# Attention scores in pieces of 32 keys on 64x32 tiles, and another order of row halves in the output products

## The chip, the cores and the metric

The kernel runs on one core of a Trainium2 chip. The metric is the device time of one execution in microseconds; the time before is the median of three runs.

## The reference

Two parts follow each other. A gated linear attention makes an output per token and head; a feed-forward block with an unusual activation takes these outputs as its input.

```python
# attention: 4 batches, 8 heads, 768 tokens, head size 48
state = zeros((B, H, D, D))
for t in range(S):
    state = alpha[:, :, t, :, None] * state + einsum('bhd,bhe->bhde', k[:, :, t], v[:, :, t])
    y[:, :, t] = einsum('bhd,bhde->bhe', q[:, :, t], state)
# feed-forward: 3072 tokens, 384 -> 2048 -> 384
x = y.transpose(0, 2, 1, 3).reshape(B * S, H * D)
h = x @ w_in
sp = maximum(h, 0) + log1p(exp(-abs(h)))
out = (h * erf(sp)) @ w_out
```

## The kernel before

**The attention** works on chunks of 64 tokens for two batches at once (NI = 2, i). There are 24 chunks; after every twelfth a new pair of batches begins. The eight heads stand as four pairs; the two heads of a pair (par) lie in the two halves of the 128 partitions, rows 0 to 47 and 64 to 111. (For the second batch the halves are swapped.) In a chunk the running product of alpha (A) goes into the queries (Q = q * A) and into the keys (K = k / A); then three groups of float32 products on TensorE do the work:

- scores, step a4, line 198: `pS = K^T Q`, 64 keys by 64 queries for each pair, batch and half: 16 products. VectorE multiplies the whole result with the causal mask (line 203) into sT.
- outputs, step a5, line 226: `py` sums, for both batches, the state's share (T with Q, 48 rows) and the chunk's own share (v with sT, 64 rows). Each product makes 32 columns of the output by 64 tokens, on a tile of 64 rows by 32 columns of TensorE's array that `tile_position=(r0, c0)` names. The row half r0 is where the operands lie; the column strip c0 is where the output lies. Heads of 48 columns are cut into pieces (PIECES) so that 32 columns fit a strip. A chunk has 64 such products, 32 where no state exists yet (the first chunk of a pair of batches).
- state updates, also in a5, line 237: `pu = k^T v`, 16 products on four 64x64 tiles, but for the last chunk of a pair of batches. Ahead of the scores, line 187 transposes K for them.

Then `put` (lines 274 and 275) turns py into the block's input x_hi and x_lo, and VectorE brings the state up to date (lines 250 to 255).

**The feed-forward** takes blocks of 256 tokens, two chunks of two batches each; there are twelve. H (line 310) makes h in float32r with three products for one (hi and lo parts), 128x128 weights by 256 tokens; U, L1, L2, G and Z are the activation, on ScalarE and VectorE; O (line 367) multiplies with w_out, 384 columns wide, into two accumulators.

**Order.** Each engine runs its instructions in program order. The order of the steps is written out by hand in three strings: START, then ORDER for each following block, then TAIL. In ORDER the attention of two coming chunks (`a1_0 ... a5_1`) is woven into the steps of this block, the block before (`@-1`) and the block after (`@1`). In steady state the scores of a chunk and its outputs are apart by half an H or more: `a4_0 H_0_0@1 ld_1 a5_0` and `a4_1 O_3_1@-1 H_2_0@1 L1_3 L2_2 H_2_1@1 a5_1`. In the scores the loop's innermost index is par, so the row half changes with each product; in the outputs it is i, with the row half `(par ^ i) * HD`, so that within four products the halves are 0, 64, 64, 0. The scores name no tile position: a product of up to 64 rows and 64 columns uses the 64x64 tile where its operands and its output lie.

Of the kernel before, what the change touches and what calls it, by code (L numbers as in the profile page):

```python
# [44 lines left out]
def gla_moe(ctx: ExitStack, tc: tile.TileContext, q, k, v, alpha, w_in, w_out, out):  # L45
    nc = tc.nc


    M, CPB, _, D, NP, NI, TC = q.shape
# [11 lines left out]
    HD = 64  # L61
# [25 lines left out]
    for i in range(NI):  # L87
        half = maskn[i * TC : (i + 1) * TC]
        nc.gpsimd.affine_select(
            out=half, in_=half, pattern=[[1, TC]], compare_op=ALU.is_ge, fill=0.0, base=0, channel_multiplier=-1  # L90
# [43 lines left out]
    class Chunk:  # L134
# [47 lines left out]
        def a4(self):  # L182
            K, Q = self.K, self.Q
            if not self.last:
                pn = ps_at.tile([P, 512], F32, name="pn", tag="at")
                for pair in range(NP):
                    nc.tensor.transpose(  # L187
                        pn[:, pair * P : (pair + 1) * P], K[:, pair].rearrange("p i t -> p (i t)"), ident
                    )
                self.kn = at.tile([P, NP, 2, HD], F32, name="kn", tag="kn", bufs=1)  # L190
                nc.scalar.activation(self.kn.rearrange("p a b d -> p (a b d)"), pn, AF.Copy)

            ps = ps_at.tile([P, NP * NI, TC], F32, name="pS", tag="at")
            for pair in range(NP):
                for i in range(NI):
                    for par in range(2):
                        rows = slice(par * HD, par * HD + D)
                        nc.tensor.matmul(  # L198
                            out=ps[par * HD : (par + 1) * HD, pair * NI + i, :],
                            lhsT=K[rows, pair, i, :], rhs=Q[rows, pair, i, :], start=True, stop=True,  # L200
                        )
            self.sT = at.tile([P, NP, NI, TC], F32, name="sT", tag="sT", bufs=1)
            nc.vector.tensor_tensor(
                out=self.sT.rearrange("p a i t -> p (a i) t"), in0=ps, in1=maskn.unsqueeze(1).broadcast_to([P, NP * NI, TC]), op=ALU.mult
            )

        def a5(self, moe):
            vx, vt = self.vv[:, : NI * NP * HD], self.vv[:, NI * NP * HD :]
            if self.n % 2 == 0:
                moe.alloc_x()  # L210

            py = [ps_at.tile([P, KT, TC], F32, name="py", tag="at") for _ in range(NI)]
            for kt in range(KT):
                sums = []
                for w, d0 in PIECES[kt]:
                    if not self.first:
                        sums.append((w, d0, T, D, self.Q))
                    sums.append((w, d0, vx, HD, self.sT))
                for n, (w, d0, left, rows, right) in enumerate(sums):
                    for part in range(2):  # L220
                        for par in range(2):
                            for i in range(NI):
                                r0, pair = (par ^ i) * HD, 2 * part + w
                                at0 = (i * NP + pair) * HD + d0
                                c0 = par * HD + part * 32
                                nc.tensor.matmul(  # L226
                                    out=py[i][c0 : c0 + 32, kt, :], lhsT=left[r0 : r0 + rows, at0 : at0 + 32],
                                    rhs=right[r0 : r0 + rows, pair, i, :], start=n == 0, stop=n == len(sums) - 1,
                                    tile_position=(r0, c0),
                                )  # L230
            if not self.last:
                pu = [ps_at.tile([P, 512], F32, name="pu", tag="at") for _ in range(NI)]
                for pair in range(NP):
                    for half in range(2):
                        for i in range(NI):
                            toks, h = slice(i * TC, (i + 1) * TC), 2 * pair + (half ^ i)
                            nc.tensor.matmul(  # L237
                                out=pu[i][half * HD : (half + 1) * HD, pair * D : (pair + 1) * D],
                                lhsT=self.kn[toks, pair, half, :], rhs=vt[toks, h * D : (h + 1) * D],
                                start=True, stop=True,  # L240
                            )
            moe.put(py, self.n % 2)
            if not self.last:
                ae = self.A[:, :, TC].rearrange("p (a i) -> p i a", a=NP)
                aeb = ae.unsqueeze(3).broadcast_to([P, NI, NP, D])
                for i in range(NI):
                    U = pu[i][:, : NP * D].rearrange("p (a d) -> p a d", a=NP)
                    if self.first:
                        nc.vector.scalar_tensor_tensor(
                            out=Tv[:, i], in0=U, scalar=-1.0, in1=aeb[:, i], op0=ALU.mult, op1=ALU.mult  # L250
                        )
                    else:
                        nc.vector.tensor_tensor(out=Tv[:, i], in0=Tv[:, i], in1=U, op=ALU.subtract)
                if not self.first:
                    nc.vector.tensor_tensor(out=Tv, in0=Tv, in1=aeb, op=ALU.mult)
# [272 lines left out]
    for i in range(1, NBLK):  # L528
# [6 lines left out]
        out=top[:, 0:2], in_=flags.rearrange("p n two -> p two n"), op=ALU.max, axis=mybir.AxisListType.X  # L535
# [67 lines left out]
```

## Time and profile before

| what | value |
|---|---|
| median of three runs | 584.02 us (581.95 to 585.95) |
| the profiled execution, its own time | 582.33 us |
| its span, from the first to the last instruction | 580.4 us |
| mean granted TensorE clock | 0.969 |
| busy: TensorE, its weight loads, VectorE, ScalarE | 90%, 85%, 83%, 81% |
| TensorE matmul records | 7386 |

The profile is of one execution. PE is TensorE's matmuls, PEld its weight loads, DVE VectorE, ACT ScalarE. A row of a group names the line, the engine, the operation, the tiles (output <- inputs), the number of records, the busy time and the mean of one. A float32 product of the code shows as two records, each a weight load and a matmul; a float32r product shows as one. The durations of records overlap, since the matmuls are pipelined: pace is read from the distance between starts. The view by stretches shows, for each stretch, its length, each engine's busy time and in parentheses the number of records that were under way in it, then the granted clock and the DMA share; where a line is named, it counts that line's records alone.

### The profile page before, as it was taken

To read this page: it belongs to the slowest core of one execution; us is meant where nothing else is said; L and a number is where in the kernel's file an instruction comes from. 1 tells how busy PE (TensorE), PEld (TensorE's weight loads), DVE (VectorE), ACT (ScalarE), POOL (GpSimd) and SP (SyncE) were. 2 spreads that over 40 slices of the span, in tenths; PEclk is the share of its full clock that TensorE was granted. 3 is DMA by queue.
4 is the path that set the end of the run, shared out by engine and by line. 5 is a ranking of instruction groups with operands and counts; after the bars stand their busy time and mean duration, and the time that the engine had idled before them with its cause. 6 is when DMAs were issued, how large, how long until landed. Compare 5 with 4: busy or idle time off the path is not lost.

```text
span 580.4 us, 16926 instructions
## 1 busy us (share of the span) xinstructions
PE 519.5 (90%) x7386; PEld 496.0 (85%) x7386; DVE 483.6 (83%) x688; ACT 468.6 (81%) x704; POOL 2.4 (0%) x16
## 2 busy tenths in 40 slices
PE   0588687499999999999999999999999999999584
PEld 0486686488989999999999999999999999999584
DVE  6779969999999979969789699699699698594970
ACT  4446799579999799699699798797896996989911
POOL 1000000000000000000000000000000000000000
PEclk9999799789999999999999999999999999999878
DMA  6575633522412222212202312221211100000000
GB/s 194 177 230 168 203 91 107 178 86 63 128 28 61 76 55 62 64 52 75 88 25 65 88 32 72 75 61 43 73 62 44 53 8 30 1 29 1 28 0 33
DMA packets 36370, 43.64 MB, mean 75 GB/s; under 512 B 21952, under 2 KB 25024, under 8 KB 36288
## 3 DMA queue, kind: packets, MB, share of 16 engines
q1 hardware_dynamic: 36288, 42.48, 24.3%
q8 instruction: 60, 0.98, 0.7%
q14 instruction: 22, 0.18, 0.1%
HBM read 37.75 MB, written 4.72 MB: 73 GB/s over the span
## 4 chain that ended last, share of the span: by engine, by line
PE 69%; DVE 15%; ACT 9%; issue 3%; DMA 2%; SPq 0%; ACTq 0%; DVEq 0%
PE acc L367 29%; PE ph L310 29%; PE py L226 4%; PE pS L198 3%; DVE wbuf L401 2%; DVE s L342 2%; ACT s L326 2%; PE pu L237 1%; PE pn L187 1%; DVE wbuf L404 1%; DVE A L156 1%; DVE t L334 1%; DVE w L335 1%; DVE hs L343 1%; ACT hs L315 1%
## 5 line engine op out<-in xcount | busy, mean ns | idle before, releaser
L310 PE MATMUL ph<-x_hi,wi_hi 128*128 128x256 f32 x576 | 166.9, 290 | 7.5 <-ACT wi_hi L379 4.8
L310 PE MATMUL ph<-x_lo,wi_hi 128*128 128x256 f32 x576 | 164.0, 285 | 0.0
L310 PE MATMUL ph<-x_hi,wi_lo 128*128 128x256 f32 x576 | 163.7, 285 | 0.3 <-DVE wi_lo L380 0.2
L367 PE MATMUL acc<-wo_hi,gh 128*128 128x384 f32 x384 | 133.2, 347 | 16.4 <-DVE gh L356 16.4
L367 PE MATMUL acc<-wo_hi,gl 128*128 128x384 f32 x384 | 131.4, 346 | 2.0 <-DVE gl L359 1.9
L367 PE MATMUL acc<-wo_lo,gh 128*128 128x384 f32 x384 | 131.0, 341 | 0.0
L310 PEld LDWEIGHTS ph<-x_hi,wi_hi 128*128 128x128 f32 x576 | 111.4, 194 | 10.1 <-ACT wi_hi L379 5.1
L359 DVE TENSOR_TENSOR gl<-hs,gh 128x512 fp32r<-128x512 f32 x96 | 64.9, 686 | 58.4 <-ACT gh L358 57.6
L310 PEld LDWEIGHTS ph<-x_hi,wi_lo 128*128 128x128 f32 x576 | 111.5, 194 | 1.0 <-DVE wi_lo L380 0.8
L310 PEld LDWEIGHTS ph<-x_lo,wi_hi 128*128 128x128 f32 x576 | 111.0, 193 | 0.5 <-DVE x_lo L275 0.3
L367 PEld LDWEIGHTS acc<-wo_hi,gh 128*128 128x128 f32 x384 | 73.8, 192 | 18.0 <-issue 8.7
L315 ACT ACTIVATE hs<-ph 128x512 f32<-128x512 f32 x96 | 56.3, 590 | 39.3 <-PE ph L310 38.1
L367 PEld LDWEIGHTS acc<-wo_hi,gl 128*128 128x128 f32 x384 | 72.7, 191 | 7.4 <-DVE gl L359 7.0
L367 PEld LDWEIGHTS acc<-wo_lo,gh 128*128 128x128 f32 x384 | 73.7, 192 | 0.0
L334 DVE TENSOR_TENSOR t<-s,w 128x1024 f32<-128x1024 f32 x48 | 58.5, 1218 | 1.9 <-ACT w L328 1.4
L335 DVE SCALAR_TENSOR_TENSOR w<-t,w 128x1024 f32<-128x1024 f32 x48 | 58.4, 1216 | 0.3
L358 ACT ACTIVATE gh<-hs 128x512 fp32r<-128x512 f32 x72 | 44.9, 625 | 16.3 <-PE acc L367 12.5
L343 DVE SCALAR_TENSOR_TENSOR hs<-s,hs 128x1024 f32<-128x1024 f32 x48 | 57.9, 1215 | 0.1
L342 DVE TENSOR_TENSOR s<-s,w 128x1024 f32<-128x1024 f32 x48 | 57.5, 1215 | 0.4 <-ACT s L338 0.4
L326 ACT ACTIVATE s<-s,fixed 128x1024 f32<-128x1024 f32 x48 | 54.6, 1141 | 0.0
L321 ACT ACTIVATE s<-hs 128x1024 f32<-128x1024 f32 x48 | 49.7, 1055 | 1.6 <-DVE wbuf L398 0.9
L328 ACT ACTIVATE w<-w 128x1024 f32<-128x1024 f32 x48 | 50.4, 1051 | 0.3
(62 smaller groups left out, 715.1 us busy)
## 6 DMA issues: line engine op xcount, KB each, us to landing
raw_v<-in_v_dram SPq DMA_DIRECT2D x24, 448.0 KB, 3.7
wst<-in_moe_w_in_dram SPq DMA_DIRECT2D x12, 512.0 KB, 5.7
wst<-in_moe_w_out_dram SPq DMA_DIRECT2D x16, 384.0 KB, 3.7
raw_a<-in_alpha_dram SPq DMA_DIRECT2D x48, 96.0 KB, 2.9
raw_k<-in_k_dram SPq DMA_DIRECT2D x48, 96.0 KB, 2.2
raw_q<-in_q_dram SPq DMA_DIRECT2D x48, 96.0 KB, 2.3
out_dram<-o SPq DMA_DIRECT2D x24, 192.0 KB, 1.9
```

Source lines behind the costliest of these rows:

```text
L310: nc.tensor.matmul(out=o, lhsT=wt[:, kt, fs], rhs=xt[:, kt, :], start=n == 0, stop=n == 3 * KT - 1)
L315: nc.scalar.activation(self.hs[g][:, sl], ph, AF.Copy)
L321: tab(nc.scalar.activation(self.s[g], self.hs[g], AF.Tanh, scale=-0.5))
L326: tab(nc.scalar.activation(s, s, AF.Ln, scale=0.5 - 2.0**-24, bias=bhalf))
L328: tab(nc.scalar.activation(w, w, AF.Exp, scale=-1.0))
L334: nc.vector.tensor_tensor(out=t, in0=s, in1=w, op=ALU.mult)
L335: nc.vector.scalar_tensor_tensor(out=w, in0=t, scalar=2.0, in1=w, op0=ALU.add, op1=ALU.mult)
L342: nc.vector.tensor_tensor(out=s, in0=s, in1=w, op=ALU.mult)
L343: nc.vector.scalar_tensor_tensor(out=h, in0=s, scalar=RT2 / 2, in1=h, op0=ALU.subtract, op1=ALU.mult)
L358: nc.scalar.activation(ghf, gg, AF.Copy)
L359: nc.vector.tensor_tensor(out=gl.rearrange("p a t -> p (a t)"), in0=gg, in1=ghf.bitcast(F32), op=ALU.subtract)
L367: nc.tensor.matmul(out=self.acc[tt][:, :DM], lhsT=gt[:, u, ts], rhs=wt[:, f, :], start=f == 0 and n == 0, stop=f == NF - 1 and n == 2,)
```

## The change

The scores are made in pieces of 32 keys. Each product of 64 keys by 64 queries becomes two of 32 by 64, with an explicit position on a 64x32 tile: rows 0 go to the column strips 0 and 32, rows 64 to the strips 64 and 96. The piece is the outer loop, the half the inner one, so that the row half still changes with each product. A chunk's scores have 32 products instead of 16. The values and their places in pS are the same.

The outputs keep their products, tiles and sums; the innermost loop now runs over the row half, and the batch follows from it. Within four products the halves are 0, 64, 0, 64 and the batches 0, 1, 1, 0.

```diff
             for pair in range(NP):
                 for i in range(NI):
-                    for par in range(2):
-                        rows = slice(par * HD, par * HD + D)
-                        nc.tensor.matmul(
-                            out=ps[par * HD : (par + 1) * HD, pair * NI + i, :],
-                            lhsT=K[rows, pair, i, :], rhs=Q[rows, pair, i, :], start=True, stop=True,
-                        )
+                    for k0 in range(0, TC, 32):
+                        for par in range(2):
+                            r0, c0 = par * HD, par * HD + k0
+                            nc.tensor.matmul(
+                                out=ps[c0 : c0 + 32, pair * NI + i, :], lhsT=K[r0 : r0 + D, pair, i, k0 : k0 + 32],
+                                rhs=Q[r0 : r0 + D, pair, i, :], start=True, stop=True, tile_position=(r0, c0),
+                            )
...
                         for par in range(2):
-                            for i in range(NI):
-                                r0, pair = (par ^ i) * HD, 2 * part + w
+                            for half in range(2):
+                                r0, i, pair = half * HD, half ^ par, 2 * part + w
                                 at0 = (i * NP + pair) * HD + d0
                                 c0 = par * HD + part * 32
```

## Prediction

> **What bounds the kernel now.** I read the page's chain first, then the chain in order of time, then busy time by stage, and last the records of the touched lines.
>
> ```profile
> PE 69%; DVE 15%; ACT 9%; issue 3%; DMA 2%; SPq 0%; ACTq 0%; DVEq 0%
> PE acc L367 29%; PE ph L310 29%; PE py L226 4%; PE pS L198 3%; DVE wbuf L401 2%; DVE s L342 2%; ACT s L326 2%; PE pu L237 1%; PE pn L187 1%; DVE wbuf L404 1%; DVE A L156 1%; DVE t L334 1%; DVE w L335 1%; DVE hs L343 1%; ACT hs L315 1%
> ```
>
> Both touched lines, L198 (scores, pS) and L226 (outputs, py), stand in the chain with 3% and 4%: 7% of the time is all that the change can act on. Where they stand in it:
>
> ```profile
> 16.39 1.93 PE pS L198 x32
> ...
> 177.28 1.08 PE pS L198 x32
> 178.36 2.25 PE ph L310 x18
> 180.61 1.41 PE py L226 x89
> ...
> 300.30 1.08 PE pS L198 x32
> 301.38 2.25 PE ph L310 x18
> 303.63 1.41 PE py L226 x89
> ...
> 478.56 1.08 PE pS L198 x32
> ...
> 486.15 1.41 PE py L226 x89
> ```
>
> From 177 to 487 us each chunk has its 1.08 us of scores and its 1.41 us of outputs in the chain: 16 of each (two per group of 256 tokens, eight groups; one outputs row, that of a batch pair's first chunk, is only 0.79 us). The one other scores row is at 16.39. In two of those stages TensorE has no gap:
>
> ```profile
> 220.00:280.00 60.00, 60.00 (x975) 58.00 (x978) 54.07 (x70) 53.52 (x79) 0.00 (x0) 1.00 0.24 68
> ...
> 400.00:460.00 60.00, 60.00 (x912) 58.09 (x911) 49.00 (x68) 49.70 (x76) 0.00 (x0) 1.00 0.20 61
> ```
>
> The second number is TensorE's busy time: 60.00 of 60. So a nanosecond saved or added per chunk counts 16 times, nearly undiluted; VectorE, next at 54 of 60, leaves room. Before 160 us the chain is mixed, and I count nothing there.
>
> **The scores.** One product in the code leaves two records, each a weight load and a matmul: L198 makes 4 pairs x 2 batches x 2 halves x 24 chunks = 384 products and has 768 records.
>
> ```profile
> L198 PEld LDWEIGHTS pS<-Q,K x768: 128/135/228, 16.3 to 479.4; 48*64 48x64 f32 x192
> L198 PE MATMUL pS<-Q,K x768: 217/219/367, 16.3 to 479.4; 48*64 48x64 f32 x192
> ...
> L226 PEld LDWEIGHTS py<-sT,raw_v x1536: 102/106/175, 19.1 to 487.3; 64*32 64x32 f32 x192
> ```
>
> A load of 64 columns lasts 135 ns and one of 32 lasts 106: 29 ns less, so I put the loading itself at about 27 ns per 32 columns (an estimate from the difference). The rest is latency, which overlaps.
>
> ```profile
> 300.23 1.15 PE L198 MATMUL pS<-Q,K 48*64 48x64 f32 x32
> 301.31 0.39 PE L310 MATMUL ph<-x_hi,wi_hi 128*128 128x256 f32 x1
> ...
> 304.98 0.68 PE L237 MATMUL pu<-raw_v,kn 64*64 64x48 f32 x32
> 305.59 0.45 PE L367 MATMUL acc<-wo_hi,gh 128*128 128x384 f32 x1
> ```
>
> The first number is a start, the second the time to the last end. Scores use two tiles, (rows 0, columns 0) and (64, 64). From the first start to the last is 1.15 - 0.22 = 0.93 us for 16 records on each tile: 58 ns per record. Then 0.15 us pass before the next stage starts. The state updates (L237) use four 64x64 tiles, two in each row half: 0.68 - 0.22 = 0.46 us for 8 records on each, again 58 ns. So four tiles run side by side, and what takes time is the turn of one tile.
>
> What sets that turn, the loading of 64 columns or the streaming of 64? The first 50 us run at half the pace, and there the two come apart. The next two fences are busy time in stretches of lines L198 and L226, and I read only the record counts (x), which grow with the end of the stretch:
>
> ```profile
> 16.30:16.64 0.34, 0.32 (x6) 0.32 (x8) 1.00 0.71 205
> 16.30:16.75 0.45, 0.43 (x8) 0.43 (x10) 1.00 0.64 182
> 16.30:16.86 0.56, 0.54 (x10) 0.54 (x12) 1.00 0.67 194
> ```
>
> ```profile
> 30.75:31.07 0.32, 0.31 (x24) 0.32 (x32) 1.00 0.99 408
> 30.75:31.18 0.43, 0.42 (x32) 0.42 (x33) 1.00 1.04 427
> 30.75:31.20 0.45, 0.44 (x33) 0.45 (x34) 1.00 1.02 418
> 30.75:31.41 0.66, 0.65 (x48) 0.66 (x50) 1.00 1.02 415
> ```
>
> Scores add one record per tile in 0.11 us, and outputs too (8 records on 8 tiles in 0.11 us), though these load only 32 columns. What the two share is the 64 moving columns. At full pace those take half, 53 ns, about what 64 weight columns take. So halving the weight columns alone gains next to nothing in a tile's turn: 58 ns can fall to about 53 to 57.
>
> The edit makes 32 products of 16, on tiles (0,0), (64,64), (0,32), (64,96): twice the tiles, twice the records, still 16 records of 64 moving columns on each. **Double the parallelism is spent on double the work.** What is left is the first load (27 ns instead of 54) and the turn. With the outputs' own pace as turn:
>
> ```profile
> 262.53:262.61 0.08, 0.07 (x8) 0.07 (x15) 1.00 0.00 0
> 262.53:262.67 0.14, 0.13 (x16) 0.13 (x23) 1.00 0.00 0
> 262.53:262.73 0.20, 0.18 (x24) 0.19 (x31) 1.00 0.00 0
> 262.53:262.79 0.26, 0.24 (x32) 0.25 (x33) 1.00 0.00 0
> 262.53:262.86 0.33, 0.32 (x33) 0.32 (x34) 1.00 0.00 0
> ...
> 262.53:263.19 0.66, 0.65 (x64) 0.65 (x64) 1.00 0.36 78
> ```
>
> Eight records, one per tile, come every 0.06 us (my stretches end 0.06 apart; I take 56 ns): 27 + 15x56 + 20 for the fourth tile's offset + 148 = 1.035 us instead of 1.08, a gain of 0.04.
>
> But the same fence shows a **break after 16 products**. 32 records are out by 0.26 us; by 0.33 us only one more has started and only one or two loads. The remaining 31 then take 0.33 us, half the pace. In the slow stretch the break has the same place: 32 records by 31.18, and the loads go 32, 33, 34 in 0.13 us, then on. I read it so: the first 16 products are laid out ahead on their tiles; after them products enter in order, and one whose tile is still busy holds up all behind it, so that its load is no longer hidden and each costs its tile 27 + 53 + 53 = 133 ns instead of 112.
>
> The old scores have exactly 16 products and never meet this; the new have 32 and should. Priced: 27 + 8x56 = 475 ns for the first four products of each tile; 20 ns until the next in line may follow, two more steps of 17 (0.33 us for 17 products is 19, with the break) and a load of 27 until the last tile starts its fifth, 81; three further turns of 133; 56 to the last record; 148 after it. Sum 475 + 81 + 399 + 56 + 148 = 1.16 us: **0.08 us more** per chunk. The bounds are -0.08 us (no break, a turn of 53) and +0.21 us (the 0.13 us in which the outputs' loads nearly stop, on top of this). I take +0.08: the row it is nearest to is another 64x32 stage of more than 16 products. 16 x 0.08 = +1.3 us; bounds -1.3 and +3.4.
>
> The mask multiply (L203) starts as much later; the outputs that need it come over 2 us behind (178.36 to 180.61), so that costs nothing. There are no new waits and no DMA.
>
> **The outputs' order.** Same 64 products, same tiles, each met again after eight; only the order of the row halves goes from 0, 64, 64, 0 to 0, 64, 0, 64. If neighbours on one half hindered each other, the old pace would be uneven within a group of four, and the full pace of the first 32 records would not be reached with that order. It is reached: 8 records per 56 ns is all that eight tiles can do. Later the count goes
>
> ```profile
> 303.55:303.88 0.33, 0.32 (x33) 0.32 (x34) 1.00 0.00 0
> 303.55:304.21 0.66, 0.65 (x66) 0.65 (x68) 1.00 0.21 50
> 303.55:304.54 0.99, 0.98 (x100) 0.98 (x102) 1.00 0.43 118
> ```
>
> 34 loads per 0.33 us, whatever the position in the group of eight. I cost the order at nothing; the bounds are -0.35 us per chunk (all 64 products at the first pace: 27 + 15x56 + 47 = 0.91 instead of 1.41 - 0.15 = 1.26) and +0.1.
>
> A rule of the Trainium skill bears on this. TensorE: Matmul & The Clock Gate, The mechanism (in Part 3), says that a weight load overlaps matmuls in flight only when their row groups differ. The state updates disagree:
>
> ```profile
> 304.96:305.05 0.09, 0.07 (x4) 0.08 (x8) 1.00 0.09 23
> 304.96:305.10 0.14, 0.12 (x8) 0.13 (x11) 1.00 0.06 15
> ```
>
> four matmuls, two in each half, have started and all eight loads with them. By that rule of the Trainium skill the new order would help and the pieces, two of which share a half, would hurt; both are priced below as mechanisms of this kernel. The same page of the Trainium skill puts TensorE's queue at 64 deep (the table at its head); 16 products are 64 loads and matmuls, which is where the break stands.
>
> **Sum.** The profiled execution took 582.33 us (span 580.4 and 1.9 around it), 1.7 below the median of 584.02. 582.33 + 1.3 + 0 = 583.6; carried to the median, **585.3 us**.
>
> **Rivals.** (a) *The pieces keep the first pace.* If 32 products on four tiles never run ahead of the line, since four tiles take one product per 28 ns and the line brings one per 19, the break may not show: 16 x -0.04 = -0.6 us, 583.4 us. For it: in the slow stretch the pace over the whole count hardly drops (16 records per 0.21 us throughout). Against: its loads do stop at the 17th product. Here the change would have done nothing.
>
> (b) *The order does lift the outputs.* If the pace after the break comes of two neighbours on one half, 15 stages gain up to 0.35 us and the short one half of it: -5.4 us; with (a) or the forecast for the scores, 578.0 or 579.9 us. Against: the even counts above; for: all of 0.35 us per chunk is lost to something.
>
> (c) *Two pieces of one half exclude each other: slower.* If a load into columns 32 waits until columns 0 of that half has streamed, each half does its 32 records in turn, 27 + 53 = 80 ns each: 2.56 us for 0.93, +1.6 us per chunk, 16 times +26: 610 us. If only the streams took turns, 32 x 56 = 1.79 us, +0.86 per chunk: 598 us. It decides the case from 0.36 us more per chunk, which is 1% over 16 chunks. Against: the four tiles of L237 at 58 ns a turn. This is what the rule quoted from the Trainium skill would do to the scores.
>
> **How the numbers follow.** About 1%, 5.8 us, is what a measurement of this kernel tells from no change. Forecast 0.42, (a) 0.26, (b) 0.18, (c) 0.10, and 0.04 for what I don't see, split evenly. The forecast and (a) lie within 1%; (b) straddles its edge (578.2), half each. Faster 0.09 + 0.02 = 0.11, slower 0.10 + 0.02 = 0.12, the same 0.77. The range from 577.5 to 589.5 holds (b) at its lower end and the bound of +3.4 us above (587.4) with some scatter (the three runs span 4 us); it leaves out (c).
>
> **What would show it.** In the changed profile: 64 records for the scores of a chunk, in 1.16 us up to the next stage (1.04 would be (a), 1.9 or more (c)); loads of about 106 ns; the first 32 records in about 0.45 us, then a slower second half; outputs still 1.41 us with 34 loads per 0.33 us; L310 and L367 unchanged, and TensorE without a gap from 177 to 487 us. Outputs of 1.1 to 1.2 us would make the prediction wrong in its second step, a chunk's scores under 1.0 us in its first.

## The result, and the profile after

The changed kernel takes 592.86 us (median of six runs, 589.12 to 595.94) against 584.26 us for the kernel before on the same chip (six runs, 581.95 to 585.95). The ratio is 1.0156, with a 95% interval from 1.0122 to 1.0189: slower by 1.6%, and above the upper end of the predicted range. The profiled execution took 592.95 us with a span of 590.9 us, 10.5 us more than the span before. (The profiled execution of before is one of the kernel's shorter ones, 1.9 us below its median; the medians are 8.6 us apart.)

The page of the changed kernel: busy time, the instruction queue among the DMA queues (packets, MB, share), and the chain's shares by engine.

```profile
PE 522.6 (88%) x8154; PEld 499.0 (84%) x8154; DVE 483.9 (82%) x688; ACT 468.8 (79%) x704; POOL 2.4 (0%) x16
...
q8 instruction: 66, 1.08, 0.8%
...
PE 70%; DVE 14%; ACT 9%; issue 4%; DMA 2%; SPq 0%; ACTq 0%; DVEq 0%
```

There are 768 records more, as the change says. "issue" has gone from 3% to 4%, and queue q8 from 60 packets to 66. Both small differences matter in what follows. The kernel before had:

```profile
q8 instruction: 60, 0.98, 0.7%
```

Now the chain in order of time (start, length, engine, tile, line, records), for one chunk in which nothing went wrong (302 us) and around the four places where something did:

```profile
221.87 1.41 PE py L227 x89
223.28 0.38 PE pu L238 x16
223.66 1.94 issue
225.60 0.45 PE pu L238 x16
...
302.01 1.03 PE pS L199 x64
...
305.30 1.41 PE py L227 x89
306.71 0.61 PE pu L238 x32
307.32 2.29 PE acc L368 x12
...
389.80 0.38 PE pu L238 x16
390.18 1.64 issue
391.81 0.45 PE pu L238 x16
...
449.71 0.48 PE pu L238 x18
450.19 1.74 issue
451.93 0.44 PE pu L238 x11
...
478.18 0.60 PE pu L238 x30
478.78 1.58 issue
480.37 0.31 PE pu L238 x2
480.68 3.83 PE acc L368 x12
```

Scores: 1.03 us where before had 1.08. Outputs: 1.41 us, unchanged. But four times TensorE **stands still** in the middle of the 32 records of a state update, with nothing to wait for that the profile shows ("issue"). The state updates last 0.61 us undisturbed and 2.77, 2.47, 2.66 and 2.49 us in these four places: 7.95 us more. The view of TensorE's waits gives the same four (total us, count, longest) and two waits of this kind at the outputs:

```profile
PE pu L238 <- issue: 6.9, 4, 1.9
PE py L227 <- issue: 1.3, 2, 1.0
```

The kernel before has one short wait of this kind, at its outputs:

```profile
PE py L226 <- issue: 0.3, 1, 0.3
```

The two at the outputs, 1.0 us at 89 us and 0.3 us at 141 us, lie ahead of 177 us, where TensorE waits for other engines too. They are not part of the loss: the first outputs of the later stretch start at 180.28 us in the changed chain and at 180.61 us before.

Two of the four are followed by a stretch in which the clock was granted at one half. In the view by stretches the column behind POOL's is the granted clock:

```profile
453.28:456.69 3.41, 3.41 (x18) 3.41 (x18) 3.31 (x7) 0.93 (x2) 0.00 (x0) 0.50 0.52 167
480.60:484.00 3.40, 3.40 (x13) 3.39 (x12) 3.40 (x7) 3.34 (x4) 0.00 (x0) 0.50 0.02 5
```

Behind the fourth the O step lasts 3.83 us instead of 2.29, 1.5 us more; 3.41 us at half speed is worth 1.7. I count 1.6 for each. The account of the span: 7.95 + 2 x 1.6 - 16 x 0.05 = 10.35 of the 10.5 us.

**Where the standstills lie.** Records on TensorE (in parentheses, first PE, then PEld) from the start to a moment inside each standstill of the state updates:

```profile
0.00:224.00 224.00, 178.45 (x3286) 166.05 (x3286) 198.12 (x318) 174.43 (x285) 2.42 (x16) 0.95 0.41 120
0.00:390.50 390.50, 343.01 (x5970) 324.86 (x5970) 339.98 (x506) 319.97 (x500) 2.42 (x16) 0.97 0.32 95
0.00:451.00 451.00, 401.38 (x6992) 381.16 (x6993) 393.00 (x575) 370.41 (x575) 2.42 (x16) 0.97 0.31 91
0.00:479.50 479.50, 428.24 (x7376) 407.01 (x7376) 412.51 (x604) 393.60 (x608) 2.42 (x16) 0.97 0.30 88
```

A record is two instructions, the load and the matmul. From the first standstill to the second are 2684 records, 5368 instructions, and with the 8 semaphore instructions that the trace has between them 5376 = 21 x 256. From the second to the third: 1023 loads, 1022 matmuls and 3 semaphore instructions, 2048 = 8 x 256. From the third to the fourth: 383 loads, 384 matmuls and 1 semaphore instruction, 768 = 3 x 256. And queue q8 carries packets of 16 KB (1.08 MB in 66); 6 more of them for 1536 more instructions is one packet for 256 instructions of 64 bytes. So TensorE's program arrives in **blocks of 256 instructions** while the kernel runs, and each standstill lies at the end of a block. The DMA view from 389.4 to 389.6 us, shortly ahead of the second standstill (390.18), shows the one packet on its way (packets, MB, share of 16 engines in that stretch):

```profile
q8 instruction: 1, 0.02, 31.7%
```

Ahead of each of the other three, too, one packet of this queue is on its way. These loads begin 0.4 to 0.8 us before TensorE stops, and TensorE goes on 2.3 to 2.6 us after the load's begin. The trace doesn't name what TensorE waits for; that it is the next block follows from the place, from the load on its way, from experiments 3 and 4, and from the start times of all loads (behind experiment 5).

A chunk's outputs are 64 products of 4 instructions, exactly 256, and they take 1.41 us: the densest code of the kernel. Call p the number of instructions of a chunk's outputs that have gone by when a block begins. This block then ends p instructions behind the outputs; for p up to 64 that is within the state updates, and its 256 instructions last only about 1.6 us. Counted in the traces for the 16 chunks from 177 us on:

```
before: 212 139 226 161  55 111 198 125 212 139 226 153 240 167 254 189
after:  147  10 [33] 160  -  238   5 124 147  10 [33] 152 175 [38] [61] 188
```

The brackets are the four standstills. The fifth chunk is the short one (32 products, 128 instructions): there the block of before that begins at 55 reaches far into slower code, and in the changed kernel no block begins in it. In the kernel before, a round of ORDER (two chunks) has 1266 instructions on TensorE, 14 short of five blocks, so p moves slowly, by 14 to 22 a round, and never comes to a value from 33 to 68 behind full outputs. The change adds 128 to a round, which makes 1394, 114 past five blocks; p jumps about, and four of 16 fall in.

### The profile page after: what moved, and what is told of

Same layout as the page of the kernel before. It is cut to its first block, busy times and chain, and to the rows that moved or that the text cites. A ratio compares the mean times of both kernels' runs of the same rounds, so it can differ in the third digit from the quotient of the medians.

```text
span 590.9 us, 18463 instructions
## 1 busy us (share of the span) xinstructions
PE 522.6 (88%) x8154; PEld 499.0 (84%) x8154; DVE 483.9 (82%) x688; ACT 468.8 (79%) x704; POOL 2.4 (0%) x16
## 3 DMA queue, kind: packets, MB, share of 16 engines
q8 instruction: 66, 1.08, 0.8%
## 4 chain that ended last, share of the span: by engine, by line
PE 70%; DVE 14%; ACT 9%; issue 4%; DMA 2%; SPq 0%; ACTq 0%; DVEq 0%
PE acc L368 31%; PE ph L311 30%; PE py L227 4%; PE pS L199 3%; PE pu L238 2%; ACT s L327 2%; DVE hs L344 1%; DVE s L343 1%; DVE wbuf L402 1%; PE pn L187 1%; DVE t L335 1%; DVE wbuf L405 1%; DVE w L336 1%; DVE A L156 1%; ACT w L328 1%
## 5 line engine op out<-in xcount | busy, mean ns | idle before, releaser
L368 PE MATMUL acc<-wo_hi,gh 128*128 128x384 f32 x384 | 134.7, 351 | 17.3 <-DVE gh L357 16.8
L368 PEld LDWEIGHTS acc<-wo_hi,gl 128*128 128x128 f32 x384 | 73.9, 194 | 6.7 <-DVE gl L360 6.3
```

Source lines behind the costliest of these rows:

```text
L368: nc.tensor.matmul(out=self.acc[tt][:, :DM], lhsT=gt[:, u, ts], rhs=wt[:, f, :], start=f == 0 and n == 0, stop=f == NF - 1 and n == 2,)
```

## The experiments

Theories: **A**, the position of block ends relative to the outputs makes the standstills; **B**, the outputs' new order does; **C**, the greater number of instructions does, wherever they lie. For the pace of the small products: **D**, the rate at which instructions reach the tiles sets it; **E**, the time that each tile is occupied does. (In the expectations the letters of rivals are set anew: in that of experiment 1, C stands for the pieces as such.)

| kernel | ratio to before | 95% interval | standstills over 1 us behind outputs, from 150 us on |
|---|---|---|---|
| the change | 1.0156 | 1.0122 to 1.0189 | 4 |
| 1, order only | 1.0006 | 0.9969 to 1.0043 | 0 |
| 2, pieces only | 1.019 | 1.0125 to 1.0255 | 4 |
| 3, change + 32 instructions ahead | 0.9992 | 0.9960 to 1.0025 | 0 |
| 4, before + 100 instructions ahead | 1.0178 | 1.0107 to 1.0249 | 4 |
| 5, change + 88 instructions ahead | 1.0153 | 1.0101 to 1.0206 | 5 |
| 6, change, ends moved with padding | 1.0042 | 1.0018 to 1.0066 | 0 (two waits of another kind) |
| 9, change, ends moved in place | 0.9971 | 0.9948 to 0.9994 | 0 |

Ahead of 150 us there are others, which the table leaves out: the longest is 1.0 us in the change, 1.1 in experiment 2, 1.5 in 4 and 1.0 in 5.

### 1. The order alone

```diff
-                            for i in range(NI):
-                                r0, pair = (par ^ i) * HD, 2 * part + w
+                            for half in range(2):
+                                r0, i, pair = half * HD, half ^ par, 2 * part + w
```

> Only the outputs' row order is changed; the scores stay in 64x64 tiles. Theory A (where a block of 256 TensorE instructions ends decides: in the changed kernel TensorE stands still four times, at instructions 256k + 193 of the trace, each time in the state updates right behind a chunk's outputs, 1.8 to 2.2 us, while the next block of instructions is still being loaded): the number of TensorE instructions per chunk is that of before, the block ends fall as before, so no standstill and 584 us (582 to 586). Rival B (the new order of the row halves makes the state updates behind it stand still): four standstills or more and about 592 us. Rival C (the pieces of the scores do it): 584 us, as A.

Measured: 585.79 us against 585.64, ratio 1.0006; a span of 583.9 us and no standstill. B falls, and the order costs and gains nothing that can be measured.

### 2. The pieces alone

```diff
-                    for par in range(2):
-                        rows = slice(par * HD, par * HD + D)
+                    for k0 in range(0, TC, 32):
+                        for par in range(2):
+                            r0, c0 = par * HD, par * HD + k0
...
```

> Only the scores are in pieces of 32 keys; the outputs keep the order 0, 64, 64, 0. Theory A: as many TensorE instructions as the changed kernel, block ends at the same places (33, 33, 38 and 61 instructions into a chunk's outputs among others), so the same four standstills and 592 to 593 us. Rival B: 583 us, without standstills. Rival C (more instructions to load, wherever the blocks end): 592 us.

Measured: 595.12 us, ratio 1.019, at least all of the change's loss and above the expected 592 to 593. Its waits, and the stretch up to the first standstill:

```profile
PE pu L238 <- issue: 7.0, 4, 1.9
```

```profile
0.00:225.00 225.00, 177.86 (x3286) 164.62 (x3286) 198.41 (x319) 174.95 (x285) 2.42 (x16) 0.95 0.40 120
```

Again 3286 records lie ahead of the first standstill, and the other three stand at the same instructions as in the change. Here three of the four are followed by 3.41 us at half clock.

### 3. The change with 32 instructions ahead of everything

```diff
+    pad = ps_at.tile([P, 512], F32, name="pad", tag="at")
+    for _ in range(8):
+        nc.tensor.matmul(out=pad[:1, :1], lhsT=maskn[:, :1], rhs=maskn[:, :1], start=True, stop=True)
     run(START, 0, 0)
```

> The changed kernel with 8 one-column float32 products (32 TensorE instructions more) ahead of everything, whose result nobody reads. They run while TensorE waits for its first data. Theory A: every block end moves 32 instructions towards the start of the code; none falls between 33 and 80 instructions into the outputs of a chunk in the stretch in which TensorE sets the time, so no standstill: 592.9 - 4 x 1.9 - 2 to 3 for the clock = 582 to 584 us. Rivals B and C (order, or amount of instructions): nothing changes, 592 to 593 us.

Eight products of one column at the very beginning, 32 instructions **more**, take the loss away: 585.0 us against 585.64, ratio 0.9992 (1 us above the expected 582 to 584). The chunk whose state updates took 2.77 us now has (chain, waits):

```profile
225.43 1.41 PE py L227 x89
226.84 0.61 PE pu L238 x32
```

```profile
PE pu L238 <- issue: 0.3, 1, 0.3
```

C falls. With 32 instructions ahead each p drops by 31: 33 becomes 2, 38 becomes 7, and both are free. 124 (twice, one of them ahead of 177 us) and 61 become 93 and 30, and cost 0.5 to 0.6 us each.

### 4. The kernel before with 100 instructions ahead

```diff
+    pad = ps_at.tile([P, 512], F32, name="pad", tag="at")
+    for _ in range(25):
+        nc.tensor.matmul(out=pad[:1, :1], lhsT=maskn[:, :1], rhs=maskn[:, :1], start=True, stop=True)
     run(START, 0, 0)
```

> The kernel before, with neither part of the change, and 25 one-column float32 products (100 TensorE instructions more) ahead of everything. Theory A: the block ends move 100 instructions, and in the stretch in which TensorE sets the time five of them now fall 40, 62, 40, 54 and 68 instructions into a chunk's outputs: five standstills of 1.3 to 2 us, with the clock that follows some of them 592 to 598 us. Rivals B and C: nothing but 25 small products more at the start, 584 to 585 us.

This is the sharpest test of A, since nothing of the change is in it. 595.17 us, ratio 1.0178: the kernel before can be made as slow as the changed one by 25 tiny products at its start. In its chain:

```profile
202.05 1.41 PE py L226 x89
203.47 0.47 PE pu L237 x19
203.94 2.18 issue
206.12 0.44 PE pu L237 x13
```

19 records, 38 instructions, behind the outputs, where p is 40. Of the five places expected, those with p of 40, 40, 54 and 68 stood still for 1.8 to 2.4 us (from one matmul's start to the next). The one with 62 cost nothing: it fell behind the last chunk of a pair of batches, which has no state updates, so that what follows the outputs is less dense. Two weak ones, 0.53 and 0.63 us, came at p of 25 and 26.

### 5. The change with 88 instructions ahead

```diff
+    def pad(n):
+        t = ps_at.tile([P, 512], F32, name="pad", tag="at")
+        for _ in range(n):
+            nc.tensor.matmul(out=t[:1, :1], lhsT=maskn[:, :1], rhs=maskn[:, :1], start=True, stop=True)
+
+    pad(22)
     run(START, 0, 0)
```

> The changed kernel with 22 of the small products (88 TensorE instructions) ahead of everything instead of 8. Theory A, as a dose: five block ends now lie 37 to 73 instructions into a chunk's outputs in the stretch in which TensorE sets the time (60, 73, 37, 60, 65), a sixth (37) at its edge and one (88) on the rim; so five or six standstills of 1.3 to 2.1 us, a weak one of 0.6, and the clock behind some: 594 to 600 us. If the changed kernel's loss had another cause, and the 8 products of e3 helped in another way, 22 should help as 8 did: 585 us.

Five standstills came, at p of 37, 60, 37, 60 and 65, and 592.6 us, ratio 1.0153: 1.4 us below the expected 594 to 600. The waits:

```profile
PE pu L238 <- issue: 8.2, 5, 2.1
PE ph L311 <- issue: 1.6, 1, 1.6
```

Four of the five at the state updates belong to them; the fifth lies ahead of 150 us (0.95 us at 108 us, p = 60). The standstill of p = 65 ended at the H product that follows the updates, and is the second line. Experiment 3 took the same single buffer for its padding, so what separates the two kernels is the number of instructions alone.

Two things speak for the lower time. A block end with p = 73 fell behind the last chunk of a pair, as in experiment 4, and cost nothing, and one with 88 cost nothing either. And only one of the five standstills was followed by a half clock.

What p cost over the traces of the change and of experiments 3 to 5, from 150 us on and behind full outputs with state updates (from one matmul's start to the next):

```
p                 up to 12   25-30     33       37-40     54-61     65, 68    88   93       99 and more
standstill, us       0      0.5-0.6   1.9-2.2   2.0-2.4   1.8-1.9     1.8     0    0.5-0.6       0
```

The start times of the loads show why. Each block has one packet of q8, in order. In all eleven traces of this case (669 blocks) TensorE began no block sooner than 2.1 us after the start of its packet, and the long standstills of the table ended 2.3 to 2.7 us after it. So it matters when the packet starts. Take the block that begins p instructions into full outputs, from 150 us on: the packet of the *next* block started 0.7 to 1.7 us before this one began for p up to 12, 0.2 to 0.7 us before for 25 to 30, and 0.7 to 2.0 us after for 33 and more. That is why the densest blocks of all, 1.41 us with p of 2 or 5, cost nothing, and why from 33 on a block must itself last some 3.4 us. With p = 88 it lasted 3.6 us, since it reached into O, whose records start 0.17 us apart; with p = 93 it reached into H, 0.12 us apart, and would have lasted 3.3.

### 6. The change, with the ends moved by padding

```diff
+    pad(6)
+    MORE = {8: 1, 9: 6}
...
+        if i in MORE:
+            pad(MORE[i])
```

> The changed kernel with 24 TensorE instructions ahead of everything, 4 ahead of the eighth and 24 ahead of the ninth round of ORDER (6, 1 and 6 small products), so that no block ends between 12 and 98 instructions into a chunk's outputs. Theory A: no standstill at all, not even those of 0.5 us that e3 had; the scores' 0.05 us per chunk are left as a gain, about 0.8 us, less 0.4 us for the small products between the rounds: 0.1% faster than before, which cannot be told from no change; 584 to 586 us by the scale of the first four runs.

A miss: 586.83 us against 583.55, ratio 1.0042. There was no standstill behind outputs, as A has it, but the padding between rounds wrote to a PSUM buffer that VectorE had not yet read, and TensorE waited for it. The waits and the timeline:

```profile
PE pad L531 <- DVE x_lo L276: 1.9, 2, 0.9
```

```profile
410.31 0.28 PE L311 MATMUL ph<-x_hi,wi_lo 128*128 128x256 f32 x1
411.50 0.19 PE L531 MATMUL pad<-maskn 128*1 128x1 f32 x2 [0.92 <-DVE x_lo L276]
```

From the start of the H product to the pad 1.2 us go by, and the same again at 453 us: 2.4 us, 0.4%, about the size of the miss (0.1% faster was expected).

### 7. The outputs over half the tokens

The kernel before, with each outputs product over 32 of its 64 tokens; the other half is copied from them, so half of the outputs' work is left out.

```diff
-                                    out=py[i][c0 : c0 + 32, kt, :], lhsT=left[r0 : r0 + rows, at0 : at0 + 32],
-                                    rhs=right[r0 : r0 + rows, pair, i, :], start=n == 0, stop=n == len(sums) - 1,
+                                    out=py[i][c0 : c0 + 32, kt, : TC // 2], lhsT=left[r0 : r0 + rows, at0 : at0 + 32],
+                                    rhs=right[r0 : r0 + rows, pair, i, : TC // 2], start=n == 0, stop=n == len(sums) - 1,
...
```

> The kernel before, but the outputs' products run over 32 of the 64 tokens and the other 32 get a copy, so half of the outputs' products is left out; the number of instructions is the same. Theory D (behind the first 16 products the rate at which the instructions come sets the pace, 17 products per 0.33 us): the outputs still need 1.25 to 1.27 us from first to last start. Rival E (the tiles set it: 27 + 53 + 53 ns for each product and tile): with 27 instead of 53 a tile's product needs 80 ns, eight tiles 10 ns per product, and the outputs need 0.7 to 0.8 us.

One execution, 584.02 us. From first to last start a chunk's outputs take 1.097 us instead of 1.268: between the two theories, nearer to D. Stretches of the outputs' line:

```profile
306.75:307.09 0.34, 0.33 (x37) 0.33 (x39) 1.00 0.00 0
306.75:307.42 0.67, 0.66 (x77) 0.66 (x79) 1.00 0.33 77
306.75:307.75 0.99, 0.98 (x117) 0.99 (x118) 1.00 0.45 124
```

40 records, 20 products, in each 0.33 us: 16.7 ns for a product, although the streaming was halved. Full outputs have 34 records in 0.33 us, 19.4 ns. So I take 16.7 of the 19.4 ns to be the price of bringing four instructions to the array; the other 2.7 depend on the size.

### 8. The scores over half the queries

The change, with each scores product over 32 of its 64 queries and the other half copied; half of the scores' work is left out.

```diff
-                                out=ps[c0 : c0 + 32, pair * NI + i, :], lhsT=K[r0 : r0 + D, pair, i, k0 : k0 + 32],
-                                rhs=Q[r0 : r0 + D, pair, i, :], start=True, stop=True, tile_position=(r0, c0),
+                                out=ps[c0 : c0 + 32, pair * NI + i, : TC // 2], lhsT=K[r0 : r0 + D, pair, i, k0 : k0 + 32],
+                                rhs=Q[r0 : r0 + D, pair, i, : TC // 2], start=True, stop=True, tile_position=(r0, c0),
...
```

> The changed kernel, but the scores' products run over 32 of the 64 queries and the other 32 get a copy, so half of the scores' products is left out; the number of instructions is the same. Four tiles now need about 30 ns per record, 15 ns per product, which is faster than the 19 ns at which instructions come behind the first 16 products. Theory D: the first 32 records take about 0.25 us, the other 32 about 0.31 us, in sum 0.55 to 0.60 us from first to last start, with the break that the full scores do not have. Without a limit of the instructions: 0.49 us, no break. The standstills behind the outputs stay as in the changed kernel.

```profile
180.13:180.72 0.59, 0.58 (x64) 0.58 (x64) 1.00 0.00 0
```

The stretches of the scores' line: 64 records are through in 0.59 us, and their starts lie within 0.563 us, on four tiles. The outputs of experiment 7's short chunk (64 records too, on eight tiles) also took 0.563 us: twice the tiles, the same time, within D's 0.55 to 0.60 and above the 0.49 without such a limit. That speaks for D. What is shown is a pace of 16.7 ns per product behind the first 16 that the number of tiles doesn't change; that it is the arrival of the instructions is the reading. With all 64 queries the starts of the same pieces lie within 0.88 us: there it is the four tiles that set the pace. The standstills stayed where the change has them (one execution, 591.7 us): taking work out of the scores without taking instructions out moves no block end.

### 9. The change, with the ends moved in place

Six tiny products (24 instructions) ahead of everything, and one score product of chunk 20 and six of chunk 22 made twice, in a buffer that they write anyway.

```diff
+            for again in range({20: 1, 22: 6}.get(self.n, 0)):
+                par, k0 = again % 2, again // 2 % 2 * 32
...
+    for _ in range(6):
+        nc.tensor.matmul(out=pad[:1, :1], lhsT=maskn[:, :1], rhs=maskn[:, :1], start=True, stop=True)
```

> As e6, with 24 TensorE instructions ahead of everything, but the 4 and the 24 in the middle are not products into a buffer of their own, for which TensorE waited 1.2 us twice in e6: one product of chunk 20's scores and six of chunk 22's are made once more, in their own place, ahead of the others. The block ends fall as in e6. Theory A: no standstill behind the outputs and no wait at the repeated products, which cost 28 ns each, 0.2 us in all; the scores' gain of 0.05 us in 16 chunks is left: 0.6 us less than before, a ratio of 0.999, not to be told from no change (the interval of e6 is 0.5% wide). If e6 was slower for another reason than the two waits, this one is 0.4% slower too.

582.59 us against 584.52, ratio 0.9971 (0.9948 to 0.9994): 0.3% below the kernel before. In the chain the chunk that began this story is whole again, and TensorE's waits on issue come to 0.8 us:

```profile
218.76 1.03 PE pS L206 x64
...
222.05 1.41 PE py L234 x89
223.46 0.61 PE pu L245 x32
```

```profile
PE py L234 <- issue: 0.8, 2, 0.5
```

The pieces' own gain, 16 x 0.05 = 0.8 us, is 0.14%; the interval holds it. What the rest of the 0.3% is, if it is more than scatter, stays open.

## Why the prediction was wrong

**The step that failed** is the sum: "583.6; carried to the median, 585.3 us", made of +1.3 us for the scores and 0 for the order. It priced the 384 additional products by their execution and gave their 1536 instructions no price as code. That left out 7.95 us of standstills and some 3.2 us of half clock behind two of them; its own term for the scores came out at -0.8 us instead of +1.3. The line that I gave as a sign, "TensorE without a gap from 177 to 487 us", is what the trace refuted. No rival had it either: all three looked for the change's effect inside the two touched lines, and it came out at a third, L238, which the diff doesn't touch. Experiments 3 and 4 show the cause: the loss goes with 32 more instructions in the changed kernel, and comes with 100 more in the unchanged one; and each standstill ends 2.3 to 2.7 us after the next block's load has begun.

Could it have been seen? The packets of queue q8 were on the page before, and a trace of before holds the instructions in order. What the trace of before did not show is a long standstill of this kind, since from 177 us on none of its ends fell into the costly range. The price was not to be read there, though the risk was.

**Step 1, the scores: wrong in sign, right in its main thought.** The forecast was +0.08 us per chunk, measured -0.05 (chain rows 1.08 and 1.03): rival (a) at 1.035 us. The stretches of the scores' line in the changed kernel show no break:

```profile
301.93:302.38 0.45, 0.44 (x32) 0.44 (x36) 1.00 0.00 0
301.93:302.61 0.68, 0.67 (x48) 0.67 (x52) 1.00 0.00 0
301.93:302.83 0.90, 0.89 (x64) 0.89 (x64) 1.00 0.00 0
```

32 records by 0.45 us, 16 more in the next 0.23 and 16 in the last 0.22, on four tiles: a turn of 56 ns where 58 stood before. The term "three further turns of 133" doesn't exist. The break in the outputs is one of supply: experiments 7 and 8 give 16.7 ns per product once the first ones are through, and full outputs on eight tiles could use one every 14 ns. Four tiles with a turn of 56 ns per record use one product per 28 ns, slower than the supply, so they never run short. That is the argument by which rival (a) was stated; I chose against it because another 64x32 stage had the break, although that stage has twice the tiles. "Double the parallelism is spent on double the work" held.

**Step 2, the outputs' order at nothing: right**, by the same 1.41 us in the chain and by experiment 1. Rival (b) is refuted, and so is (c): two pieces in each half ran at a turn of 56 ns. The rule quoted from the Trainium skill (TensorE: Matmul & The Clock Gate, The mechanism), by which the one would help and the other hurt, is not borne out here by either. The 64-deep queue that the same page of the Trainium skill names fits the first 16 products of 4 instructions; no run here shows the queue itself.

**Loads of 106 ns:** right. The scores' loads of the changed kernel have a median of 107 ns (three numbers: least, median, most):

```profile
L199 PEld LDWEIGHTS pS<-Q,K x1536: 102/107/174, 16.2 to 489.5; 48*32 48x32 f32 x192
```

**Still open:** what makes the next block's load start ahead of the running block for p up to 30, and only some time into it from 33 on; why the clock falls to a half after some standstills only (2 of 4 in the change, 3 of 4, 1 of 4 and 1 of 5 in experiments 2, 4 and 5); and what the 2.7 ns per product are by which full outputs are slower than the supply (in the trace they too bring 8 records in 0.067 us, and lose some 0.045 us once in 32).

## What to carry to other kernels

An edit that multiplies small instructions has two prices: the pace at which they execute, and where they push the block ends of all code behind them. When time appears as "issue" at a line that the diff doesn't touch, count instructions between the gaps; if the distances are multiples of 256, add a few harmless instructions at the start before judging the edit, since a loss that padding removes is not the edit's own. Splitting a product's weight columns over twice the tiles, with the moving columns of each piece the same, gained only 0.05 of 1.08 us here.

## What the runs showed of the hardware

- TensorE's instructions are brought in while the kernel runs, 256 (16 KB) at a time. No block began sooner than 2.1 us after the start of its load. A load that starts 0.8 us or more into a dense block, one whose instructions execute in about 1.6 us, comes too late; TensorE then stands still for up to 2.4 us, as an "issue" with no releaser. The blocks with such a standstill lasted 3.4 to 4.1 us from one end to the next.
- Whether that happens hangs on alignment: 32 instructions at the start of the program removed 1.6% of the time, 100 added 1.8%.
- Float32 products of 32 moving columns, four instructions each, follow each other every 16.7 ns behind the first 16, whether they go to four tiles or eight (64 records in 0.563 us in both).
- A standstill of 1.6 to 2.2 us can be followed by 3.41 us at a granted clock of 0.50: 7 of the 17 in the table of experiments were, the other ten were not.
